# A second matmul stage dealt out in five equal parts of paired half-array matmuls

## The chip, the cores and the metric

One core of one Trainium2 chip. Times are device microseconds (us) of one execution; medians and ranges are over several executions (four of each kernel, unless said otherwise). Engines go by the profile's names: PE is TensorE (matmuls), ACT ScalarE, DVE VectorE, POOL GpSimd, and SP the one that issues most DMAs. PSUM is the memory that matmuls write.

## The reference, cut to what matters

A causal convolution with 7 taps per head (a softmax over the taps) runs along a sequence; its result y goes through a feed-forward layer with a maximum of three branches:

```python
x   = conv(x, softmax(weight))                # (8, 4160, 192), 8 heads of 24 channels
h   = max(max(x @ w1, x @ w2), x @ w3)        # (33280, 768)
out = h @ w_out                               # (33280, 192)
```

The kernel works on 65 tiles of 512 tokens and uses max(a, b, c) = c + max(relu(a - c), b - c): the first stage makes y @ (w1 - w3) in `lp` and y @ (w2 - w3) in `lq`, h is max(relu(lp), lq), and the second stage gives h @ w_out + y @ (w3 @ w_out), with w3 @ w_out prepared once as `m16`.

## The kernel before

TensorE is split into two halves of 64 rows: rows 0 to 63 ("half 0") and 64 to 127 ("half 1") hold different work and run side by side. A first-stage tile l1(j) is three pairs of 64-row matmuls, lp on half 0 and lq on half 1. ACT takes lp out of PSUM (`r`), and DVE takes lq and r into `h`. lp and lq have two PSUM buffers each, so l1(j) needs the buffers of l1(j-2) back. Three words recur below: a *slot* is the 0.083 us by which successive second-stage matmuls of one half follow each other, the *lag* is how far the first lq of an l1 starts behind its first lp, and conv(n) is the convolution of tile n, four tiles ahead of the l1 around it.

```python
def l1(t, j):                                  # j = 0..5
    ps = [pool.tile([P, NBLK], FP32, tag=tag, ...) for pool, tag in ((psp, "p"), (psq, "q"))]
    for c in range(NC):                        # NC = 3
        for i in range(2):                     # half 0 -> lp, half 1 -> lq
            nc.tensor.matmul(ps[i][:, 0:N], lhsT=wd[row, c, P*j:P*(j+1)], rhs=y[row, c, ...], ...)
    nc.scalar.activation(out=r[:, 0:N], in_=ps[0][:, 0:N], func=AF.Relu)
    nc.vector.tensor_max(out=hs[t][:, j, 0:N], in0=r[:, 0:N], in1=ps[1][:, 0:N])

def st2(t, s):                                 # one of four token tiles: 8 matmuls on one half, 7 on the other
    ...
for t in range(NB):
    load_x(t + AHEAD + 2); cast_x(t + AHEAD + 1)     # AHEAD = 4; the cast runs on POOL
    l1(t, 0)
    conv(t + AHEAD)                                  # 40 matmuls, then ACT casts the two banks G to ys
    repack(t + AHEAD)                                # every 2nd tile: 10 pieces ys -> yd (SP), then yd -> yd (POOL)
    l1(t, 1)
    for j in range(2, NJ):                           # NJ = 6
        st2(t - 1, j - 2)
        l1(t, j)
    store(t - 1)                                     # a DMA issued by POOL
```

The softmax here doesn't subtract the row's maximum and nothing guards it: scores larger than these inputs give would overflow.

## Time and profile before

| | before |
|---|---|
| time, median (range) | 539.17 us (539.09 to 540.47), three runs; a fourth, added later, makes it 539.18 |
| span in the profile | 537.5 us |
| period of the loop | 7.382 us |
| conv(5) to conv(64), 59 periods | 436.66 us |
| of that beyond 59 x 7.382 | 1.1 us |
| tile without a conv (the last four) | 7.08 us |

A busy share says little here. What carries the argument is when each matmul *starts*. Conv starts make a clean clock for the period, because conv uses the whole array and waits for both halves. The prediction below shows the lines.

### The profile page before, as it was taken

Reading aid. Unit: us, or ns where it says so; the run is one execution under the profiler, and the core shown is the slowest. Engines: PE = TensorE matmul, PEld = TensorE weight load, DVE = VectorE, ACT = ScalarE, POOL = GpSimd, SP = SyncE. Lnnn points to the kernel's source line nnn. Section 1 sums busy time; section 2 is a strip of 40 time slices with the busy share of each in tenths; the row PEclk is TensorE's granted clock in tenths of the full one; section 3 lists DMA queues with packets and bytes.
Section 4 is the critical chain, followed back from the end, with each engine's and each line's share of the span. In section 5 each row is a group of like instructions: output and inputs, shape, how many; then the busy total and the mean of one; then the engine's idle time right before and its main releaser. Section 6 shows DMA issues by size and latency. Waiting matters only on the chain.

```text
span 537.5 us, 21248 instructions
## 1 busy us (share of the span) xinstructions
PE 491.3 (91%) x8906; PEld 348.1 (65%) x8906; DVE 337.7 (63%) x542; ACT 362.0 (67%) x654; POOL 143.4 (27%) x205
## 2 busy tenths in 40 slices
PE   0084999999999999999999999999999999999993
PEld 0072766677666777666776766776667766667773
DVE  1322666766766667667667677666676666776772
ACT  1133677777777777777777777777777777776661
POOL 1132223333332221233333332221333333313113
PEclk9996999999999999999999999999999999999997
DMA  7735566666665654666666656655666666634412
GB/s 178 196 77 151 129 172 191 186 189 188 188 185 141 178 172 129 183 190 185 185 193 184 182 153 175 176 160 145 187 189 187 186 192 185 171 101 121 129 60 60
DMA packets 65751, 87.72 MB, mean 163 GB/s; under 512 B 7592, under 2 KB 51304, under 8 KB 65656
## 3 DMA queue, kind: packets, MB, share of 16 engines
q1 hardware_dynamic: 54648, 47.36, 33.1%
q0 software_dynamic: 10224, 38.28, 24.6%
q8 instruction: 70, 1.15, 0.9%
q10 hardware_dynamic: 784, 0.72, 0.4%
q14 instruction: 25, 0.20, 0.1%
HBM read 34.93 MB, written 25.85 MB: 113 GB/s over the span
## 4 chain that ended last, share of the span: by engine, by line
PE 86%; DMA 6%; ACT 2%; SPq 2%; POOL 1%; DVE 1%; issue 1%; ACTq 1%; POOLq 0%
PE lp L273 32%; PE po L303 29%; PE lq L273 18%; PE G L222 7%; DMA Rd<-taps 2%; SPq L259 2%; DMA bandc<-Rd 1%; DMA Rd<-zero 1%; ACTq L255 1%; DVE h L278 1%; ACT r L277 1%; DMA yd<-ys 1%; DMA xf<-in_x_dram 1%; POOL out_dram L322 1%; POOL x L133 1%
## 5 line engine op out<-in xcount | busy, mean ns | idle before, releaser
L278 DVE TENSOR_TENSOR h<-r,lq 128x512 f16<-128x512 f16 x390 | 268.3, 688 | 163.3 <-ACT r L277 150.6
L273 PE MATMUL lq<-yd,wd 64*128 64x512 f16 x1170 | 316.5, 377 | 2.0 <-DVE h L278 2.0
L273 PE MATMUL lp<-yd,wd 64*128 64x512 f16 x1170 | 316.3, 378 | 0.0
L277 ACT ACTIVATE r<-lp 128x512 f16<-128x512 f32 x390 | 234.0, 600 | 117.6 <-PE lp L273 89.0
L303 PE MATMUL po<-wo,h 64*128 64x192 f16 x3120 | 182.9, 243 | 0.7 <-DVE h L278 0.7
L273 PEld LDWEIGHTS <-wd 64*128 64x128 f16 x2340 | 129.4, 94 | 79.2 <-issue 36.4
L303 PEld LDWEIGHTS <-h 64*128 64x128 f16 x3120 | 144.4, 94 | 1.0 <-DVE h L278 0.9
L260 POOL DMA_DIRECT2D yd<-yd x33 | 18.1, 550 | 306.2 <-DMA yd<-ys 146.8
L231 ACT CAST ys<-G 128x512 f16<-128x512 f32 x130 | 69.8, 589 | 26.1 <-PE G L222 17.3
L303 PE MATMUL po<-m,yd 64*128 64x192 f16 x780 | 86.5, 243 | 0.0
L303 PEld LDWEIGHTS <-yd 64*128 64x128 f16 x780 | 59.7, 94 | 39.8
L133 POOL CAST x<-xf 128x960 f16<-128x960 f32 (+3 forms) x88 | 68.5, 795 | 30.2 <-DMA xf<-in_x_dram 30.2
L222 PEld LDWEIGHTS <-x 128*32 128x32 f16 (+2 forms) x2624 | 36.9, 98 | 60.7 <-issue 41.3
L222 PE MATMUL G<-band,x 128*32 128x122 f16 (+3 forms) x2624 | 43.5, 212 | 35.2 <-DVE band L186 25.1
L308 DVE TENSOR_TENSOR o<-a,po 128x384 f32<-128x384 f32 x130 | 71.1, 547 | 2.1 <-ACT a L307 2.1
L307 ACT COPY a<-po 128x384 f32<-128x384 f32 x130 | 62.3, 479 | 2.6 <-PE po L303 2.4
L317 POOL DMA_DIRECT2D out_dram<-o x64 | 49.2, 769 | 49.8 <-PE lp L273 26.8
L187 ACT COPY band<-bandc 128x536 f16<-128x536 f16 x1 | 2.6, 2563 | 17.5 <-DMA bandc<-Rd 17.5
L183 DVE TENSOR_TENSOR wd<-ws,w3s 128x768 f16<-128x768 f32 x3 | 2.7, 954 | 12.2 <-DMA w3s<-in_moe_w_dram 12.2
L205 PE MATMUL pm<-wos,w3t 128*128 128x192 f32 x24 | 5.7, 411 | 0.0
L205 PEld LDWEIGHTS pm<-wos,w3t 128*128 128x128 f32 x24 | 5.4, 252 | 0.1
L322 POOL DMA_DIRECT2D out_dram<-o x8 | 4.2, 537 | 2.0 <-DVE o L308 2.0
(20 smaller groups left out, 17.9 us busy)
## 6 DMA issues: line engine op xcount, KB each, us to landing
out_dram<-o POOLq DMA_DIRECT2D x64, 384.0 KB, 5.7
xf<-in_x_dram SPq DMA_DIRECT2D x48, 480.0 KB
yd<-yd POOLq DMA_DIRECT2D x31, 384.0 KB, 6.2
yd<-ys SPq DMA_DIRECT2D x186, 48.0 KB
xf<-in_x_dram SPq DMA_DIRECT2D x16, 384.0 KB
yd<-ys SPq DMA_DIRECT2D x62, 32.0 KB
ws<-in_moe_w_dram SPq DMA_DIRECT2D x2, 576.0 KB
w3s<-in_moe_w_dram SPq DMA_DIRECT2D x2, 576.0 KB
```

The lines of the kernel that those rows point to most:

```text
L133: nc.gpsimd.tensor_copy(out=x16[0:rl, q0:q1, :], in_=xf[0:rl, q0:q1, :])
L205: nc.tensor.matmul(ps[:], lhsT=w3t[:, j, P * i:P * (i + 1)], rhs=wos[:, j, :], start=(j == 0), stop=(j == NJ - 1))
L222: nc.tensor.matmul(G[h // 4][32 * g:32 * g + 32, lo:hi], lhsT=x16[0:rlen, q, cb:cb + 32], rhs=band[0:rlen, h, cc:cc + hi - lo], start=True ...
L231: nc.scalar.copy(out=slots[g][:, i, NBLK * k:NBLK * k + N], in_=G[i][:, 0:N])
L260: nc.gpsimd.dma_start(out=yd[HALF:P, :, w], in_=yd[0:HALF, :, w])
L273: nc.tensor.matmul(ps[i][:, 0:N], lhsT=wd[row, c, P * j:P * (j + 1)], rhs=y[row, c, NBLK * k:NBLK * k + N], start=(c == 0), stop=(c == NC ...
L277: nc.scalar.activation(out=r[:, 0:N], in_=ps[0][:, 0:N], func=AF.Relu)
L278: nc.vector.tensor_max(out=hs[t][:, j, 0:N], in0=r[:, 0:N], in1=ps[1][:, 0:N])
L303: nc.tensor.matmul(ps[i][:, s % 2, :], lhsT=todo[i][n][0], rhs=todo[i][n][1], start=(n == 0), stop=(n == len(todo[i]) - 1))
L307: nc.scalar.copy(out=a[:], in_=ps[0][:])
L308: nc.vector.tensor_add(out=outs[t][:, s - 1:s + 1, :], in0=a[:], in1=ps[1][:])
L317: nc.gpsimd.dma_start(out=out[g0:g0 + n, :].rearrange("(s p) c -> p s c", p=P), in_=ob[:])
```

## The change

Two intents in one edit. The 60 second-stage matmuls of a tile become two lists of 30, one for each half, so that each matmul has a partner on the other half. The lists are cut into five equal parts of six pairs, and one part follows each of l1(1) to l1(5), so that no two first-stage tiles are left back to back except l1(0) and l1(1), which have conv between them.

```diff
-    def st2(t, s):
+    NU = 5
+    def st2(t, u):
 ...
-        for n in range(NJ + 2):
-            for i in range(2):
-                if n < len(todo[i]):
-                    nc.tensor.matmul(ps[i][:, s % 2, :], lhsT=todo[i][n][0], rhs=todo[i][n][1], ...)
+        if u == 0:                       # two lists of 30 over the four token tiles
+            ...
+                    todo[i] += [(s, n == 0, n == len(mm) - 1, m) for n, m in enumerate(mm)]
 ...
+        n = len(todo[0])
+        for e in range(n * u // NU, n * (u + 1) // NU):
+            for i in range(2):
+                s, first, last, (a, b) = todo[i][e]
 ...
+                nc.tensor.matmul(ps[s // 2, i][:, s % 2, :], lhsT=a, rhs=b, start=first, stop=last)
 ...
-        l1(t, 1)
-        for j in range(2, NJ):
-            st2(t - 1, j - 2)
-            l1(t, j)
+        for j in range(1, NJ):
+            l1(t, j)
+            st2(t - 1, j - 1)
```

More of the change, by code (lines that the diff above doesn't have):

```diff
@@ L286, in st2 @@
         hT, y = hs[t], dense[g]
-        if s % 2 == 0:
-            halves[t] = [psw.tile([P, 2, D], FP32, tag="w", name=f"po{i}_{t}_{s}")
-                         for i in range(2)]
-        ps = halves[t]
-        tok = slice(NBLK * k + P * s, NBLK * k + P * (s + 1))
-        todo = []
-        for i in range(2):
-            row = slice(HALF * i, HALF * (i + 1))
-            mm = [(y[row, i, tok], m16[row, 0, :])]
-            if s % 2 == i:
-                mm.append((y[row, 2, tok], m16[row, 1, :]))
-            mm += [(hT[row, j, P * s:P * (s + 1)], wo[row, j, :]) for j in range(NJ)]
-            todo.append(mm)
@@ L300, in st2 @@
-        for n in range(NJ + 2):
-            for i in range(2):
-                if n < len(todo[i]):
-                    nc.tensor.matmul(ps[i][:, s % 2, :], lhsT=todo[i][n][0], rhs=todo[i][n][1],
-                                     start=(n == 0), stop=(n == len(todo[i]) - 1))
-        if s % 2 == 1:
-            a = tp.tile([P, 2, D], FP32, tag="a", name=f"a_{t}_{s}")
-            nc.scalar.copy(out=a[:], in_=ps[0][:])
-            nc.vector.tensor_add(out=outs[t][:, s - 1:s + 1, :], in0=a[:], in1=ps[1][:])
+        if u == 0:
+            todo = [[], []]
+            for s in range(4):
+                tok = slice(NBLK * k + P * s, NBLK * k + P * (s + 1))
+                for i in range(2):
+                    row = slice(HALF * i, HALF * (i + 1))
+                    mm = [(y[row, i, tok], m16[row, 0, :])]
+                    if s % 2 == i:
+                        mm.append((y[row, 2, tok], m16[row, 1, :]))
+                    mm += [(hT[row, j, P * s:P * (s + 1)], wo[row, j, :]) for j in range(NJ)]
+                    todo[i] += [(s, n == 0, n == len(mm) - 1, m) for n, m in enumerate(mm)]
+            halves[t] = (todo, {})
@@ new lines, in st2 @@
+        todo, ps = halves[t]
+        n = len(todo[0])
+        for e in range(n * u // NU, n * (u + 1) // NU):
+            for i in range(2):
+                s, first, last, (a, b) = todo[i][e]
+                if (s // 2, i) not in ps:
+                    ps[s // 2, i] = psw.tile([P, 2, D], FP32, tag="w", name=f"po{i}_{t}_{s}")
+                nc.tensor.matmul(ps[s // 2, i][:, s % 2, :], lhsT=a, rhs=b, start=first, stop=last)
+            s, _, last, _ = todo[1][e]
+            if last and s % 2 == 1:
+                a = tp.tile([P, 2, D], FP32, tag="a", name=f"a_{t}_{s}")
+                nc.scalar.copy(out=a[:], in_=ps[s // 2, 0][:])
+                nc.vector.tensor_add(out=outs[t][:, s - 1:s + 1, :], in0=a[:], in1=ps[s // 2, 1][:])
@@ L342 @@
         repack(t + AHEAD)
-        l1(t, 1)
-        for j in range(2, NJ):
-            st2(t - 1, j - 2)
+        for j in range(1, NJ):
             l1(t, j)
+            st2(t - 1, j - 1)
         store(t - 1)
-    for s in range(4):
-        st2(NB - 1, s)
+    for u in range(NU):
+        st2(NB - 1, u)
     store(NB - 1)
```

## The prediction

> **What bounds the kernel now.** I read the page's busy shares, then the chain that ended last, then one tile in order of time.
>
> ```profile
> PE 491.3 (91%) x8906; PEld 348.1 (65%) x8906; DVE 337.7 (63%) x542; ACT 362.0 (67%) x654; POOL 143.4 (27%) x205
> PE 86%; DMA 6%; ACT 2%; SPq 2%; POOL 1%; DVE 1%; issue 1%; ACTq 1%; POOLq 0%
> PE lp L273 32%; PE po L303 29%; PE lq L273 18%; PE G L222 7%; DMA Rd<-taps 2%; SPq L259 2%; DMA bandc<-Rd 1%; DMA Rd<-zero 1%; ACTq L255 1%; DVE h L278 1%; ACT r L277 1%; DMA yd<-ys 1%; DMA xf<-in_x_dram 1%; POOL out_dram L322 1%; POOL x L133 1%
> ```
>
> TensorE (PE) is the bound; ACT and DVE are two thirds busy. But "busy" is a union of matmul windows of 377 ns, while successive ones of a half start 215 ns apart, so it can hide gaps. Hence the starts. A period of the loop is l1(0), conv, l1(1), then four times [st2, l1]. Here is its end (l1(5), then l1(0) of the next tile, then conv), from the timeline of PE (start, us):
>
> ```profile
> 259.81 0.38 PE L273 MATMUL lp<-yd,wd 64*128 64x512 f16 x1
> 259.81 0.38 PE L273 MATMUL lq<-yd,wd 64*128 64x512 f16 x1
> ...
> 260.46 0.38 PE L273 MATMUL lp<-yd,wd 64*128 64x512 f16 x1
> 260.80 0.37 PE L273 MATMUL lq<-yd,wd 64*128 64x512 f16 x1
> 260.81 0.39 PE L273 MATMUL lp<-yd,wd 64*128 64x512 f16 x1
> 261.02 0.37 PE L273 MATMUL lq<-yd,wd 64*128 64x512 f16 x1
> 261.03 0.38 PE L273 MATMUL lp<-yd,wd 64*128 64x512 f16 x1
> 261.23 0.37 PE L273 MATMUL lq<-yd,wd 64*128 64x512 f16 x1
> 261.54 0.65 PE L222 MATMUL G<-band,x 128*32 128x122 f16 x40
> ```
>
> The first lq of l1(0) starts 0.34 us after its lp, where elsewhere the two start together. Two first-stage tiles stand back to back there, lq has two buffers, and this one still holds l1(4)'s result. The timelines of DVE and ACT, same tile:
>
> ```profile
> 260.06 0.69 DVE L278 TENSOR_TENSOR h<-r,lq 128x512 f16<-128x512 f16 x1 [0.62 <-ACT r L277]
> ```
>
> DVE starts that eviction at 260.06; the lq starts 0.74 later. Conv to conv is 254.15 to 261.54; averaged over many tiles the period is 7.38 us, and the 0.34 recurs in every one, though PE's idle column shows only 2.0 us in all.
>
> The other half of the argument is the eviction after conv:
>
> ```profile
> 254.85 1.07 ACT L231 CAST ys<-G 128x512 f16<-128x512 f32 x2
> 255.81 0.61 ACT L277 ACTIVATE r<-lp 128x512 f16<-128x512 f32 x1
> ```
> ```profile
> 256.46 0.69 DVE L278 TENSOR_TENSOR h<-r,lq 128x512 f16<-128x512 f16 x1 [1.00 <-ACT r L277]
> ```
> ```profile
> 255.39 0.33 PE L303 MATMUL po<-m,yd 64*128 64x192 f16 x3
> 255.97 0.38 PE L273 MATMUL lq<-yd,wd 64*128 64x512 f16 x1
> 256.05 0.38 PE L273 MATMUL lp<-yd,wd 64*128 64x512 f16 x1
> 257.28 0.38 PE L273 MATMUL lp<-yd,wd 64*128 64x512 f16 x1
> 257.28 0.38 PE L273 MATMUL lq<-yd,wd 64*128 64x512 f16 x1
> ```
>
> ACT casts the two conv banks first, so r of l1(1) waits for them, its h starts at 256.46, and the lq buffer is free at 256.46 + 0.74 = 257.20. l1(3) takes it at 257.28: 0.08 to spare.
>
> **What the Trainium skill says.** "TensorE: Matmul & The Clock Gate", Part 3 (The mechanism): matmuls on different row groups of the array run concurrently. The trace agrees: two 64-row matmuls start within 0.01 us. The same part ("What overlaps and what doesn't") says matmuls start in program order; here lq starts at 255.97 and lp, which comes before it in the program, at 256.05. So each half runs its own line of work, and a half that has one matmul fewer moves on. "TensorEngine Tiling (Array Packing)", Key Properties: changing the tiling mode drains TensorE. Agreed: conv, on 128x32 tiles, starts 0.09 us after the last lq has streamed (261.23 + 0.215 to 261.54), so it waits for the later half. "Perfetto Trace Analysis", Optimization Strategy: a gap that repeats on the engine that should be saturated can mean too few PSUM buffers. That is the 0.34.
>
> **The change, part by part.**
> 1. Pairing. Before, each st2 has 8 matmuls on one half and 7 on the other; after, 30 and 30 per tile, dealt in sixes. Counted as slots that is 32 against 30, 2 x 0.083 = 0.17 us per tile. But the half with 8 alternates: after st2(0) lp is 0.08 late, after st2(1) the two are level (257.28/257.28). Two periods of [l1, st2] take 257.93 - 255.39 = 2.54 us = 2 x 0.647 + 15 x 0.083, which is 15 slots and not 16. Nothing is lost, so pairing gains 0.
> 2. Spreading. Same instructions, other order: l1(0), conv, l1(1), u0, l1(2), u1, l1(3), u2, l1(4), u3, l1(5), u4. u4 now separates l1(5) from the next l1(0). Removed: the wait of 0.34. Conv remains between l1(0) and l1(1).
> 3. The price. A part is 6 x 0.083 = 0.50 us where st2 averaged 0.62, so l1 tiles come sooner. I walk one tile, time from the start of conv, with the durations above: l1(1) 0.59 (254.74 - 254.15); u0 1.24; l1(2) 1.74; u1 2.38; l1(3) 2.88. Evictions: ys 0.70 (254.85 - 254.15); r(1) 1.66; h(1) 2.31; lq free at 3.05. The lq of l1(3) therefore waits 3.05 - 2.88 = 0.17. lp goes on: its second matmul is due at 2.88 + 0.215 = 3.10, after the blocked lq has issued. So half 1 trails by 0.17 up to the next conv, which waits for it. The later ones: r starts 0.41 after the last lp of its l1 starts (256.49 to 256.90 in that trace), h 0.63 after r. h(2) 3.20, lq free 3.94, l1(4) takes it at 4.02; h(3) 4.35, free 5.09, taken from 5.16; h(4) 5.49, free 6.23, taken by the next l1(0) at 6.31. All pass, most by about 0.1. The output copies fit: the second runs on ACT from 6.58 to 7.03, before r(0) at 7.15.
> 4. Period after: from lq's 3.05, four l1 and three parts, 4 x 0.647 + 18 x 0.083 = 4.08, and 0.09 of drain: 7.22 us. Against 7.38 this saves 0.166; conv(5) at 54.52 to conv(64) at 491.18 are 59 periods: 9.8 us.
> 5. Data path given back. In every second tile conv needs a cast that waits in POOL's order behind the yd copy, which waits for the pieces:
>
> ```profile
> 257.94 0.55 POOL L260 DMA_DIRECT2D yd<-yd  x1 [9.32 <-DMA yd<-ys]
> 258.47 0.78 POOL L317 DMA_DIRECT2D out_dram<-o  x1
> 259.26 1.00 POOL L133 CAST x<-xf 128x960 f16<-128x960 f32 x1
> ```
>
> The cast ends 1.28 us before conv at 261.54. Over the 30 such places that slack goes from none (convs at 172.95, 438.75, 483.80, which cost some 1.1 us now) to 1.77. The chain starts at conv two tiles earlier, so it does not shrink with the period: each slack loses 2 x 0.166 = 0.33. Summing what falls below zero (0.33 at the three that already wait, 0.27 at 217.24, 0.03 at 202.48) gives 1.3 us.
> 6. Tail. The four last tiles have no conv. Before, l1(5), l1(0) and l1(1) were adjacent and a tile took 7.08 us. After, only l1(0) and l1(1) are: h(5) at 6.63 frees lq at 7.37, where lp of l1(1) is due at 6.95; its second matmul follows at 7.38 instead of 7.17, so half 0 loses 0.21: 30 slots and six l1 (6.37) + 0.21 = 6.58. Three such periods give 1.5 us. In the last st2, h(5) now ripens behind u4 and u0 (before: st2 resumed 527.42 - 518.77 = 8.65 us after that tile's l1(0), after: about 7.64): 1.0 us. Together 2.5 us.
>
> Startup up to conv(5) is untouched. Sum: 539.17 - 9.8 + 1.3 - 2.5 = 528.2 us, a ratio of 0.980.
>
> **Rivals.**
> - A: no new wait at l1(3). For: before, the same buffer had slack, and 0.17 is a small difference between sums. Then the period is 7.05, 59 x 0.33 = 19.5 saved, some 2.5 more of cast waits than now: 520 us. Against: the chain conv, ys, r, h, lq is measured link by link, and no link moves with the order.
> - B: pairing counts after all, 2 slots x 64 tiles = 10.6 us more: about 518. Against: 2.54 us for 15 slots.
> - C: loading becomes the bound. POOL and SP move the same bytes in a shorter period; were the casts' slack to vanish in most places, the time would stay near 536. For: three places already touch zero. Against: the mean slack is about 1 us and the loss 0.33.
> - D: half 1's lag hurts the other half through the common issue order, or further l1 tiles miss their buffer by the 0.1 left: each 0.05 us per tile costs 3 us, so 531 to 534. Against: in the tail before, lq runs 0.20 behind lp and lp keeps its 2.53 per pair.
>
> **Range and chances.** The estimate lies on the 2% line (528.4). The wait at l1(3) is known to about 0.04 us, 2.4 us over 59 tiles; the cast waits to about 1.5 us; C and D pull upward, A downward. Range 524 to 532. Faster 0.5, same 0.49, slower 0.01.
>
> **What would show it.** In the timeline of the changed kernel: lp and lq of l1(0) start together (step 2); lq of l1(3) 0.17 behind lp, and the lag lasts to conv (step 3); conv to conv 7.22 us (step 4); POOL's cast ends nearer to conv, with more waits of conv for x (step 5); 6.58 us between the last tiles' stores (step 6). I am wrong if lq of l1(3) does not wait (A), if parts of six pairs take clearly other than 0.50 us (B), if many periods are irregular (C), or if the lag grows from l1 to l1 (D).

## The result, and the profile after

| | before | after |
|---|---|---|
| time, median (range) | 539.18 us (539.09 to 540.47) | 530.16 us (529.13 to 531.17) |
| span in the profile | 537.5 us | 527.4 us |
| period of the loop | 7.382 us | 7.210 us |
| conv(5) to conv(64) | 436.66 us | 429.19 us |
| of that beyond 59 periods | 1.1 us | 3.8 us |
| tile without a conv | 7.08 us | 6.59 us |

The ratio is 0.9827 (95% interval 0.9803 to 0.9851). Ratios here are the mean time of one kernel's fast runs over that of the other's of the same rounds, so not quite the ratio of the medians. The gain is clear of noise and just short of 2%. The output is correct.

From the page of the changed kernel, engines' busy time and the chain that ended last, by engine:

```profile
PE 481.8 (91%) x8906; PEld 359.9 (68%) x8906; DVE 336.6 (64%) x542; ACT 356.7 (68%) x654; POOL 143.1 (27%) x205
PE 76%; DMA 8%; SPq 5%; POOL 3%; issue 3%; ACT 2%; ACTq 1%; DVE 1%; POOLq 0%
```

PE's share of the span is the same 91%, so it could not have told anything. The chain has moved: PE from 86% to 76%, and DMA, SP's queue and POOL together from 9% to 16%. Loading now ends more of the waits.

One tile from the timeline of PE (start, us): conv, l1(3), the next l1(0), the next conv.

```profile
258.10 0.65 PE L222 MATMUL G<-band,x 128*32 128x122 f16 x40 [0.36 <-POOL x L133]
...
260.98 0.38 PE L273 MATMUL lp<-yd,wd 64*128 64x512 f16 x1
261.15 0.37 PE L273 MATMUL lq<-yd,wd 64*128 64x512 f16 x1
...
264.41 0.38 PE L273 MATMUL lp<-yd,wd 64*128 64x512 f16 x1
264.49 0.24 PE L309 MATMUL po<-wo,h 64*128 64x192 f16 x1
264.57 0.38 PE L273 MATMUL lq<-yd,wd 64*128 64x512 f16 x1
...
265.31 0.65 PE L222 MATMUL G<-band,x 128*32 128x122 f16 x40
```

The 0.34 at l1(0) is gone. At l1(3) lq starts 0.17 behind lp; the lag is still 0.16 at l1(0), where half 1 does a last `po` matmul while half 0 is on lp already, and conv takes up the sum. 265.31 - 258.10 = 7.21. What frees that lq, from the timelines of ACT and DVE:

```profile
258.80 1.07 ACT L231 CAST ys<-G 128x512 f16<-128x512 f32 x2 [0.59 <-PE G L222]
259.76 0.62 ACT L277 ACTIVATE r<-lp 128x512 f16<-128x512 f32 x1
```
```profile
260.40 0.69 DVE L278 TENSOR_TENSOR h<-r,lq 128x512 f16<-128x512 f16 x1 [1.47 <-ACT r L277]
```

Counted from conv at 258.10: casts 0.70, r(1) 1.66, h(1) 2.30, lq 3.05. This is the walk of the prediction, link by link.

The same conv also shows the other wait: it stood 0.36 us for its x. From the timeline of POOL:

```profile
255.74 0.54 POOL L260 DMA_DIRECT2D yd<-yd  x1 [9.74 <-DMA xf<-in_x_dram]
256.27 0.78 POOL L323 DMA_DIRECT2D out_dram<-o  x1
257.05 0.99 POOL L133 CAST x<-xf 128x960 f16<-128x960 f32 x1
```

POOL sat 9.74 us before the yd copy could be issued; the cast behind it ended at 258.04, and conv started at 258.10. This line names a load of x as what came last, where the prediction's line named the pieces; over the changed run 17 of the copy's waits name the one and 14 the other. The copy reads the pieces and nothing of x, so what held it is not shown by this line; whether the casts wait because of the copy's place in POOL's order is tested below.

Where the 10.1 us of span went: start to conv(5) 54.52 to 54.21, -0.3; 59 periods, 59 x (7.382 - 7.210) = -10.1; casts, 3.8 - 1.1 = +2.7; from conv(64) to the end, 46.32 (537.50 - 491.18) to 43.95 (527.35 - 483.40), -2.4. Together -10.1. The profiled execution was the quickest of the four (529.13), 1.0 us below their median.

### The profile page after: what moved, and what is told of

Read it like the earlier page. It is cut to its first block, busy times and chain, and to the rows that moved or that the text cites. A ratio compares the mean times of both kernels' runs of the same rounds, so it can differ in the third digit from the quotient of the medians.

```text
span 527.4 us, 21248 instructions
## 1 busy us (share of the span) xinstructions
PE 481.8 (91%) x8906; PEld 359.9 (68%) x8906; DVE 336.6 (64%) x542; ACT 356.7 (68%) x654; POOL 143.1 (27%) x205
## 4 chain that ended last, share of the span: by engine, by line
PE 76%; DMA 8%; SPq 5%; POOL 3%; issue 3%; ACT 2%; ACTq 1%; DVE 1%; POOLq 0%
PE po L309 26%; PE lp L273 23%; PE lq L273 21%; PE G L222 6%; SPq L259 5%; DMA yd<-ys 3%; DMA Rd<-taps 2%; DMA xf<-in_x_dram 2%; POOL x L133 1%; DMA bandc<-Rd 1%; DMA Rd<-zero 1%; ACTq L255 1%; ACT r L277 1%; ACT ys L231 1%; DVE h L278 1%
## 5 line engine op out<-in xcount | busy, mean ns | idle before, releaser
L309 PE MATMUL po<-wo,h 64*128 64x192 f16 x3120 | 230.3, 243 | 0.2 <-DVE h L278 0.2
L309 PEld LDWEIGHTS <-h 64*128 64x128 f16 x3120 | 189.8, 94 | 29.5 <-DVE h L278 0.4
L273 PEld LDWEIGHTS <-wd 64*128 64x128 f16 x2340 | 148.9, 94 | 51.5 <-issue 13.7
L309 PE MATMUL po<-m,yd 64*128 64x192 f16 x780 | 96.6, 243 | 0.0
L309 PEld LDWEIGHTS <-yd 64*128 64x128 f16 x780 | 58.2, 94 | 14.6
L205 PE MATMUL pm<-wos,w3t 128*128 128x192 f32 x24 | 6.9, 474 | 0.0
L205 PEld LDWEIGHTS pm<-wos,w3t 128*128 128x128 f32 x24 | 6.6, 298 | 0.1
```

Source lines behind the costliest of these rows:

```text
L273: nc.tensor.matmul(ps[i][:, 0:N], lhsT=wd[row, c, P * j:P * (j + 1)], rhs=y[row, c, NBLK * k:NBLK * k + N], start=(c == 0), stop=(c == NC ...
L309: nc.tensor.matmul(ps[s // 2, i][:, s % 2, :], lhsT=a, rhs=b, start=first, stop=last)
```

## The experiments

Twelve kernels ran, all correct, in three lots; the kernel before, run beside each lot, had a median of 539.46, 539.89 and 539.58 us. "Period" is the median of the conv-to-conv times. My theory: the gain is the 0.34 us wait removed by spreading, less a new 0.17 us wait at l1(3), and conv's waits for x come from POOL's order of issue. The rivals: the pairing gained by saving slots of TensorE; the lag is due to the short parts as such; x arrives late whatever the order.

### Pairing alone, spreading alone

Pairing alone: the paired lists, cut in four, at the four old places.

```diff
-    NU = 5
+    NU = 4
-        for j in range(1, NJ):
-            l1(t, j)
-            st2(t - 1, j - 1)
+        l1(t, 1)
+        for j in range(2, NJ):
+            st2(t - 1, j - 2)
+            l1(t, j)
```

> The pairing alone: the second stage as one list of 30 pairs, cut into four parts that stand where the old ones stood, so l1(5) and the next l1(0) are again back to back. If spreading is what gained: the lq of l1(0) again waits 0.34 us, the period is 7.38 us and the time 539 us (537.5 to 540.5). If pairing gained (two slots of 0.083 us per tile): about 529 us and a period of 7.2 us.

Measured: 534.98 us (533.62 to 535.50), ratio 0.9916, period 7.300. A miss for both: neither nothing nor two slots.

Spreading alone: the old order of matmuls within each token tile, cut into five parts of 12.

```diff
-            halves[t] = (todo, {})
+            rows = [[[e for e in todo[i] if e[0] == s] for i in range(2)] for s in range(4)]
+            flat = [(i, r[i][n]) for r in rows for n in range(NJ + 2) for i in range(2) if n < len(r[i])]
+            halves[t] = (flat, {})
 ...                              # and a loop over flat in place of the pairs
```

> The spreading alone: the matmuls in the old order (8 on one half and 7 on the other per token tile), cut into five parts of 12 matmuls in the new places. If spreading is what gained: as the changed kernel, 530 us (529 to 532), period 7.21 us. If pairing gained: 537 us or more.

Measured: 532.66 us (531.14 to 533.89), ratio 0.9876, period 7.291. Between the two expectations again.

The four periods:

| | four old places | five places |
|---|---|---|
| unpaired | 7.382 | 7.291 |
| paired | 7.300 | 7.210 |

Each part is worth 0.08 to 0.09 us a tile by itself, and here they add. That is no rule: as the next lines show, the slot that pairing wins works on a different wait in each column. So the prediction's sentence "pairing gains 0" was wrong. The timeline of PE in the kernel with pairing alone shows how:

```profile
257.95 0.38 PE L273 MATMUL lp<-yd,wd 64*128 64x512 f16 x1
258.21 0.37 PE L273 MATMUL lq<-yd,wd 64*128 64x512 f16 x1
...
258.94 0.65 PE L222 MATMUL G<-band,x 128*32 128x122 f16 x40
```

The wait of l1(0) is still there, but 0.26 us and no longer 0.34. In the kernel before, half 0 did the eighth matmul of st2(2), so lp of l1(4) came one slot (0.083 us) late, r and h of l1(4) with it, and h(4) is what frees lq of l1(0). With pairing, l1(4) stands behind 22 slots instead of 23. No slot of TensorE is saved; an eviction starts one slot earlier.

If that is so, the same paired list cut one slot later must lose the gain. The edit to the kernel with pairing alone is the cut:

```diff
-        for e in range(n * u // NU, n * (u + 1) // NU):     # 0, 7, 15, 22, 30
+        for e in range(CUTS[u], CUTS[u + 1]):               # 0, 7, 15, 23, 30
```

> The paired stream at the four old places, but cut 7, 8, 8, 7, so that the lp of l1(4) stands behind 23 slots, as it did before the change, and 7 slots instead of 8 follow it up to the lq that needs its buffer. If the pairing gained 0.082 us a tile in the four-part kernel because l1(4) came one slot earlier and its eviction with it: lag of l1(0) back to 0.34 us, period 7.38 us, 539 us (537.5 to 540.5). If it gained because it saves slots of TensorE: period 7.30 us and 535 us, wherever it is cut.

Measured: 539.15 us (538.19 to 540.09), ratio 0.9997 (0.9968 to 1.0025), period 7.382. Its timeline of PE:

```profile
259.91 0.38 PE L273 MATMUL lp<-yd,wd 64*128 64x512 f16 x1
260.25 0.37 PE L273 MATMUL lq<-yd,wd 64*128 64x512 f16 x1
...
260.98 0.65 PE L222 MATMUL G<-band,x 128*32 128x122 f16 x40
```

The 0.34 is back, with every matmul paired. That settles it for the four places: pairing as such gains nothing, and the place of the cut gains 0.08. In the five-place kernel the slot works on the other end. Unpaired, the first 24 of the 60 matmuls give half 1 only 11 slots before its wait at l1(3), so 19 are left behind the wait; paired it is 12 and 18. This second half is counted and has no run of its own, but the traces agree with it: lq of l1(3) starts 3.05 us after conv in both kernels, and the lag at the next l1(0) is 0.25 unpaired and 0.17 paired. The walk in the prediction had put 18 there, so its total was right although its sentence was not; that was luck and not insight.

### Is a fifth place needed?

Four places again, but cut so that 11 slots follow l1(4):

```diff
+    CUTS = (0, 7, 15, 19, 30)
```

> The paired stream at the four old places, cut 7, 8, 4, 11, so that l1(4) is evicted before the next l1(0) needs its buffer. If only the distance from l1(4) counts, the wait is gone: period 7.05 us, about 520 us. By the walk it is not: l1(5), l1(0), conv and l1(1) are still in a row, l1(1) now comes 1.97 us after l1(5) and needs 2.21, so lq of l1(1) trails by 0.25 us, the period stays at 7.30 us and the time at 535 us; only a fifth place between l1(5) and l1(0) removes it.

Measured: 529.26 us (528.53 to 530.12), ratio 0.9804. Both expectations missed: periods mostly alternate between 7.08 and 7.24, 7.16 on the mean, apart from waits for x. The lag at l1(1) is there (0.21 us where 0.25 was expected), but I had stopped the walk after one tile. The lag is still 0.19 at the next l1(0), so it delays conv, and with it the next l1(1), which then comes late enough after l1(5) to wait only 0.05. One lag pays for two tiles. (The profiled run, 530.12, also lost some 5 us to waits for x.) So four places with the right cut do as well as five, and the number of places is not what counts.

### What makes lq of l1(3) wait

ACT's second conv cast (and the repack that needs it) moved behind r of l1(1):

```diff
-        conv(t + AHEAD)
-        repack(t + AHEAD)
+        evict = conv(t + AHEAD, split=True)       # casts G[0] only
         for j in range(1, NJ):
             l1(t, j)
+            if j == 1:
+                if evict:
+                    evict(1)
+                repack(t + AHEAD)
             st2(t - 1, j - 1)
```

> The changed kernel with ACT's second conv cast moved behind r of l1(1), so that r(1) waits for one cast and not for two. If the two casts ahead of r(1) cause the 0.17 us by which lq of l1(3) trails: lp and lq of l1(3) start together, the period is 7.05 us, 59 x 0.16 = 9.4 us gained and some 3 to 4 us of that lost to conv waiting for its x casts: 524 us (521.5 to 527). If the lag comes from the parts being short as such, it stays, and the time with it at 530 us.

Measured: 521.43 us (518.65 to 522.72), ratio 0.9662, period 7.046, no lag in any l1 of the loop. The timeline of ACT, with conv starting at 254.03:

```profile
254.73 0.59 ACT L233 CAST ys<-G 128x512 f16<-128x512 f32 x1
255.47 0.60 ACT L282 ACTIVATE r<-lp 128x512 f16<-128x512 f32 x1 [0.15 <-PE lq L278]
255.97 0.58 ACT L233 CAST ys<-G 128x512 f16<-128x512 f32 x1
```

r(1) starts 1.44 after conv instead of 1.66, h(1) follows it at 256.10 (2.07 in place of 2.30), and 2.07 + 0.74 = 2.81 lies ahead of the 2.88 at which l1(3) comes. The two casts ahead of r(1) were the cause.

The same from the other side: leave ACT alone, and let l1(3) come two slots later by uneven parts.

```diff
+    CUTS = (0, 8, 14, 19, 25, 30)
```

> The changed kernel with uneven parts of 8, 6, 5, 6 and 5 pairs. l1(3) then comes 2 x 0.083 us later after conv, at the moment its lq buffer comes free, and every other l1 keeps 11 slots, which with one l1 in between is the 2.21 us that an lq buffer takes. Lag 0 to 0.03 us, period 7.05 us, 524 us (521.5 to 527) as in the kernel with the cast moved. If the even cut costs nothing, that is if the lag does not delay conv: 530 us.

Measured: 522.68 us (521.36 to 523.57), ratio 0.9684, period 7.054, lags of at most 0.01 us in most tiles. Both ways remove the same 0.16, so the lag did delay conv in full. Waits for x took 6.7 us of the profiled run here and 2.0 of that of the kernel with the cast moved, which was the quickest of its four.

### What makes conv wait for x

In the changed kernel the yd copy is issued by POOL ahead of the next cast, and POOL stands until the copy can go. Issue it behind the next cast:

```diff
-        nc.gpsimd.dma_start(out=yd[HALF:P, :, w], in_=yd[0:HALF, :, w])
+        later.append(lambda: nc.gpsimd.dma_start(out=yd[HALF:P, :, w], in_=yd[0:HALF, :, w]))    # later = [] above
 ...
         cast_x(t + AHEAD + 1)
+        while later:
+            later.pop()()
```

> The changed kernel with the yd copy issued behind the next x cast in POOL's order, so that no cast waits for the pieces to land. If that order is what makes conv wait for x: period 7.21 us in every tile, no period longer by over 0.1 us, and the 3.9 us of such waits in the profiled run gone: 526 us (525 to 527.5). If x itself arrives late, or the transfers are the limit, the long periods stay and so does 530 us.

> Both cures: the second conv cast behind r of l1(1), and the yd copy behind the next x cast. No lag, period 7.05 us and no long period: 59 x 0.16 = 9.6 us below the kernel with the copy alone moved: 517 us (515.5 to 519). If POOL's order does not matter: 521 us, as with the cast alone.

> The kernel before with the yd copy behind the next x cast. Its waits of conv for x came to 1.1 us in the profiled run, so 538 us (537 to 539) if POOL's order makes them; the period stays 7.38 us. This says how much of the later gains was there to be had without the change.

Measured: 534.81 (0.9919), 526.20 (0.9755) and 548.65 us (1.0171), each 9 to 11 us above what was expected. The periods were as hoped, 7.209, 7.046 and 7.383, but conv(5) came at 62.5 to 62.7 us instead of 54.2, the period after it was 1.1 to 2.0 us too long, and the first two kernels had one more long period each (0.54 and 0.26). The waits of PE in the first of the three:

```profile
PE lq L274 <- DMA yd<-yd: 7.8, 1, 7.8
```

One wait of 7.8 us. At the start there is no earlier tile to hide behind: the copy for the second tile, which the changed kernel issues at 43.28, now went out at 51.63 together with that of the next group, and l1 waited for it. That is a fault of my edit, and these times do not settle the question. Mended by issuing the copies of the first groups where they were:

```diff
         later.append(...)
+        if t < AHEAD + 1:
+            later.pop()()
```

> The changed kernel with the yd copy behind the next x cast, but only in the loop: the copies of the first groups are issued where they were, since the run without that exception lost 8.3 us before conv(5). Conv(5) back at 54.2 us, period 7.21 us, no long periods: 526 us (525 to 527.5). If the casts' order is not the cause of the long periods: 530 us.

Measured: 525.12 us (524.67 to 525.43), ratio 0.9731. Conv(5) at 53.74, conv(64) at 479.05, which is 425.31 = 59 x 7.209: no long period is left. The timeline of POOL:

```profile
250.00 0.99 POOL L133 CAST x<-xf 128x960 f16<-128x960 f32 x1
253.28 0.54 POOL L261 DMA_DIRECT2D yd<-yd  x1 [2.29 <-issue]
```

The copy comes after the cast, and the cast no longer waits for it. From the waits view of the loop alone (us in total, times, longest), conv's weight loads waiting for casts, in the changed kernel and then here:

```profile
PEld L222 <- POOL x L133: 10.9, 16, 1.6
```
```profile
PEld L222 <- POOL x L133: 0.4, 1, 0.4
```

Part of these waits passes beside matmuls still running, so the total is above the 3.8 us lost; what counts is that 16 became one. The DMA engines were busier in the loop (0.67 against 0.63), so the transfers were not the limit. POOL's order of issue was.

The same edit in the kernel before:

> The kernel before with the yd copy behind the next x cast in the loop alone. Period 7.38 us, its 0.4 to 1.1 us of long periods gone: 538.5 us (537 to 539.5), the same within 0.5%.

Measured: 537.99 us (537.67 to 538.53), ratio 0.9971, period 7.381. There was only 1 to 2 us to be had before (1.1 by the profiled run's waits, 1.6 by the medians). The shorter period is what turned this order into a cost of 4 to 5 us, as far as an estimate can show it: for each kernel without this edit, the profiled run's time beyond 59 periods plus what its median lay above that run, gives 1.0 and 1.4 us at a period of 7.38 (before; cut 7, 8, 8, 7), 2.1 and 2.2 at 7.30 and 7.29, 4.8 at 7.21, and 4.7 and 5.8 at 7.05.

### Both cures

> Both cures with the copies of the first groups left in place: conv(5) at 54.2 us, no lag, period 7.05 us, no long periods: 517.5 us (516 to 519). If the order of the casts does not matter: 521 us, as with the cast alone.

Measured: 516.08 us (515.51 to 516.32), ratio 0.9562 (0.9543 to 0.9582), period 7.046, 0.4 us beyond 59 periods. This beats both kernels: 14 us below the changed one by the medians.

## Why the prediction was right or wrong

The time, 530.16, lies in the range and 2.0 us above the 528.2; the ratio was given as 0.980 and is 0.983. The profiled run, at 529.13, is 0.9 above: casts +1.4 against what was forecast, periods -0.3, start -0.3, tail +0.1. So what was missed in it is the casts' term; the other 1.0 is how far the median lies above the profiled run.

- **Step 1, pairing gains 0: wrong.** It rested on counting slots, and the count was right (the cut at 23 slots gives 0.9997). But it overlooked that lp of l1(4) came a slot late before, and that this reached the very wait of step 2. By itself the paired list with its cut is worth 0.082 us a tile. The total was not hurt, by luck, since step 3 walked the paired parts.
- **Step 2, the wait at l1(0) goes: right.** Spreading without pairing already removes it, though an unpaired list leaves 0.25 us of lag there, handed on from l1(3) and one more slot.
- **Step 3, a new wait of 0.17 at lq of l1(3), carried to conv: right.** 0.17 in the timeline, at 3.05 after conv as walked; the cause is shown by two experiments that take it away from opposite sides.
- **Step 4, period 7.22: right**, 7.210; 59 periods saved 10.1 and not 9.8.
- **Step 5, casts cost 1.3 more: the term that was mis-sized.** The profiled run shows 2.7 more, and moving the copy gained 5.0 us by the medians, some 0.5 of which came before conv(5). The mechanism was right. The size was taken from the slacks of one execution of the kernel before, as if each place kept its own in the changed one. It did not: the conv at 157.86 had 1.55 us of slack before, and the conv of the same tile after, at 156.42, lost 1.05. Nor is it chance alone: conv(19), (21), (33), (35) and (49) all waited in the changed kernel, in the one with spreading alone and in the one cut 7, 8, 4, 11, while the kernel with the cast moved waited at other tiles but for conv(21). What makes the copy late at one place and not at another stays open.
- **Step 6, the tail gains 2.5: right**, 2.4, with 6.59 us a tile where 6.58 was walked.
- **Rivals.** A (no new wait) falls: the wait is there; taking it away as well gives the 7.05 named for it. B falls: no slots are saved. C was underrated: loading did not become the bound, but took back over a quarter of the 59 periods' gain in the profiled run. D falls: in all tiles of the loop but one the lag stays between 0.16 and 0.18 from l1(3) to the next l1(0) and does not grow.

## What to carry to other kernels

When two row groups of the array run their own streams, follow each buffer from the start of the matmul that fills it to the start of the one that needs it again (here 2.21 us: 0.43 to the third matmul, 0.41 to r, 0.63 to h, 0.74 to the next lq), and place the work so that every such distance is met; one slot of 0.083 us in the right place was worth 5 us over the run, and a whole extra place was not needed. Put latency-bound work ahead of bulk work on the evicting engine: one cast moved on ACT was worth as much as the whole change. After each gain look at what only just kept up before, and don't carry its slack at one place over to the changed kernel.

## What the Trainium skill lacked or had wrong

- "TensorE: Matmul & The Clock Gate", Part 3 (What overlaps and what doesn't), and "PSUM — Partial Sum Buffer" (Engine vs sequencer instructions) say that matmuls start in program order. Between row groups the recorded starts here do not: before the change lq starts at 255.97 and lp, ahead of it in the program, at 256.05; after it, lp of l1(0) starts at 264.41 and a half-1 matmul of the part ahead of it at 264.49. In the changed kernel half 1 keeps a lag of 0.16 to 0.18 us from l1(3) to the next l1(0), while half 0 goes from the one (260.98) to the other (264.41) in 3.43 us, which is three l1 and 18 slots without a wait.
- "TensorEngine Tiling (Array Packing)", Key Properties, says that a change of tiling mode drains TensorE and gives no time. Here 0.09 us lay between the last 64-row matmul's streaming and the first 128x32 one, and conv starts behind the half that lags.
- "Perfetto Trace Analysis", Optimization Strategy, names repeated bubbles as a sign of too few buffers, but the page's way of seeing them, gaps on the engine, would miss these: the 0.34 us per tile were hidden under matmul windows of 377 ns, and PE's idle column showed 2.0 us for lq in the whole run. Start times of matmuls showed them.
- No page that was searched gives the turnaround of a PSUM buffer between TensorE, ACT, DVE and TensorE: 0.41 us from the start of the last matmul to r, 0.63 to h, 0.74 to the next matmul.
